# Two attention and MLP layers on one core: part of the softmax exponentials computed on VectorE

## The chip, the cores and the metric

The kernel runs on one core of a Trainium2 chip. The metric is the device time of one launch in microseconds (us). Five engines work side by side, each through its own queue in order: TensorE (PE) multiplies matrices, ScalarE (ACT) evaluates functions such as exp and gelu, VectorE (DVE) does elementwise arithmetic, GpSimd (POOL) does small helpers, and SyncE (SP) starts the DMAs. Data lie in SBUF, results of matmuls in PSUM, which has 8 banks of 128 x 512 fp32. Engines wait for each other through semaphores.

## The reference

One sequence of 2048 tokens with 512 features passes twice through the same two blocks, with the same weights both times. Block A is attention with 32 query heads of 16 features that share one key head and one value head. Block B is a mixer that shifts four quarters of the features along the sequence, and an MLP of width 1792.

```python
def _A_ref(x, wq, wk, wv, wo):
    q = (x @ wq).reshape(B, S, H, Dh).transpose(0, 2, 1, 3)      # H = 32, Dh = 16
    k = x @ wk
    v = x @ wv
    scores = jnp.einsum("bhqd,bkd->bhqk", q, k) * (Dh ** -0.5)
    p = _softmax(scores, axis=-1)
    o = jnp.einsum("bhqk,bkd->bhqd", p, v)
    return o.transpose(0, 2, 1, 3).reshape(B, S, H * Dh) @ wo

def _B_ref(x, w1, w2, w3, w4):
    h = _gelu(_layernorm(x) @ w1)
    hs = (the four quarters of h, shifted by 1, -1, 2, -2 tokens) @ w2
    x1 = x + hs
    return x1 + _gelu(_layernorm(x1) @ w3) @ w4

x = x + _A_ref(_layernorm(x), ...);  x = x + _B_ref(_layernorm(x), ...)    # and both once more
```

The softmax takes 2 x 32 x 2048 x 2048 exponentials, 268 million, for few multiplications around each of them.

## The kernel before

**Tiles and loops.** Queries are taken in four chunks of 512 per layer, heads in eight blocks of four, keys in 16 blocks of 128. One step is a *group*: layer, chunk, head block, key block, written `(la, c, b, kb)` in `make_groups` (line 582). There are 1024 groups. A group has four *tiles*, one for each head of the block: 128 keys by 512 queries of scores. So there are 4096 tiles. A score matmul (line 623) uses only 32 of the 128 rows of TensorE, at row position 32 x head. The four products with the values (line 695) use 32 columns each and run side by side into the accumulator bank 5. The values have a column of ones, so the same products also sum the exponentials. After the last key block of a head block `block_end` (line 704) copies the accumulator to SBUF, takes reciprocals and scales.

**PSUM.** ScalarE has two slots, banks 0 to 2 and banks 3 and 4. `declare_unit` (line 628) fills a slot with three or two tiles and runs one exponential over the whole slot (line 646), into one of four output buffers `EA`. Bank 5 is the accumulator. Banks 6 and 7 are a pool for everything else: projections, transposes, the mixer and the MLP. This *side work* of a chunk (`chunk_end`, line 804) is declared when its attention is done, and it runs during the attention of the chunk after it.

**Who sets the order.** The whole program is planned before it is emitted. `Plan.op` records an operation with its engine, what it reads and writes, a duration and a priority. `Plan.run` simulates the engines with those durations, and puts on each engine the ready operation with the lowest priority number. `Plan.emit` then writes each engine's queue in that order, with the semaphore waits that the dependences need. So at run time the order of every queue is fixed. An operation with `take` needs a free pool bank when it is placed; `give` returns the bank. Score units have priority 0, products with the values 2, normalisation 5, side work 10.

**The feed.** `pump` (line 757) is called as the planned clock advances. While fewer than three of the last four units are unfinished, it opens the next group, puts its tiles on a list and declares units from that list. A group's products are declared as soon as all its four tiles have a place in a unit.

**The switch.** `USE_DVE_EXP` (line 289) is False. It is read in two places. In `memory` (line 344) it allocates the buffers `DJ`, `DF`, `DG` and `ED`. In `pump` (line 770) it calls `consider_pairs` (line 791) when a group is opened, which may call `declare_pair` (line 653). With False neither function runs, and all four tiles of each group go to ScalarE.

Of the kernel before, what the change touches and what calls it, by code (L numbers as in the profile page):

```python
# [281 lines left out]
class Kernel:  # L282
# [3 lines left out]
    ACC = 5  # L286
    POOL_BANKS = (6, 7)
    N_EA = 4
    USE_DVE_EXP = False
    AHEAD = 4  # L290
    MAX_PAIRS = 2

# [7 lines left out]
    def sb(self, name, shape, dtype=dt.bfloat16):  # L300
        n = 1
        for s in shape:
            n *= s
        ap = self.stack.enter_context(self.nc.sbuf_tensor(name, [128, n], dtype))[:, :]
        self.sbytes += n * dt.size(dtype)
        return self.shaped(ap, shape)
# [9 lines left out]
    def memory(self):  # L316
# [26 lines left out]
        self.EA = sb("EA", [self.N_EA, 3, 512])  # L343
        if self.USE_DVE_EXP:
            self.DJ = sb("DJ", [2, 1024], dt.uint16)
# [411 lines left out]
    def pump(self, now):  # L757
# [5 lines left out]
        while True:  # L763
# [4 lines left out]
            while len(self.open_tiles) < nb and self.gi < G:  # L768
                n = self.gi
                if self.USE_DVE_EXP:  # L770
                    self.consider_pairs(now, n)
# [251 lines left out]
```

## Time and profile before

| | |
|---|---|
| time, median of 3 runs | 2240.59 us (2235.44 to 2243.05) |
| time of the profiled execution | 2245.48 us |
| its span, first to last instruction | 2243.3 us |
| mean granted clock of TensorE | 0.69 |
| ScalarE busy | 1990.5 us, 89% |
| TensorE busy | 1864.3 us, 83% |
| VectorE busy | 485.5 us, 22% |
| GpSimd busy | 65.7 us, 3% |

"Busy" is the time in which at least one instruction of the engine runs; on TensorE, whose matmuls are pipelined and overlap, a busy engine need not be at its peak. The granted clock is the share of TensorE's full clock that the chip allowed; the same matmul takes longer at 0.5 than at 1.0. A line of costly instructions gives the source line, engine and operation, the shapes, the count, then busy time and mean duration in nanoseconds of one, then the idle time of the engine just before them and what ended it. A line of a stretch gives its start and end, its length, the busy time of PE, weight loads, DVE, ACT and POOL with counts, the granted clock, the DMA share and GB/s. A line in order of time gives the start, the duration, the engine, the source line and the count of instructions merged in it.

### The profile page before, as it was taken

How to read it: one execution, taken by the hardware profiler on the slowest of the kernel's cores; microseconds unless marked ns; L12 is line 12 of the kernel's file. 1: busy time of each engine (PE TensorE's matmuls, PEld its weight loads, DVE VectorE, ACT ScalarE, POOL GpSimd, SP SyncE). 2: the span in 40 equal slices, each digit the busy share in tenths (PEclk: the TensorE clock that was granted, in tenths of full speed). 3: DMA queues.
4: the chain of work that ended last, by engine and by line, in shares of the span. 5: the costliest groups of instructions: out<-in, count | busy, mean ns of one | idle time of the engine just before them, and what ended most of it. 6: DMA issues, size and time to landing. Idle time of an engine off the chain costs nothing.

```text
span 2243.3 us, 26540 instructions
## 1 busy us (share of the span) xinstructions
PE 1864.3 (83%) x11836; PEld 490.0 (22%) x11836; DVE 485.5 (22%) x931; ACT 1990.5 (89%) x1699; POOL 65.7 (3%) x133
## 2 busy tenths in 40 slices
PE   6777898878888798887879789887888878887867
PEld 2111122211222122221222122221122212221123
DVE  6000032201422024210232124200142002310033
ACT  2999998999999998999999989899998999899931
POOL 3000000000000000000000000000000000000000
PEclk9555597755886578855689568765597756695568
DMA  4000000000000000000000000000000000000000
GB/s 142 1 1 1 1 1 1 1 1 1 1 1 1 1 1 1 1 1 1 1 1 1 1 1 1 1 8 1 1 1 1 10 1 1 1 8 3 1 1 12
DMA packets 10145, 11.68 MB, mean 5 GB/s; under 512 B 1584, under 2 KB 9520, under 8 KB 10032
## 3 DMA queue, kind: packets, MB, share of 16 engines
q1 hardware_dynamic: 10032, 10.00, 1.4%
q8 instruction: 92, 1.51, 0.3%
q14 instruction: 21, 0.17, 0.0%
HBM read 7.90 MB, written 2.10 MB: 4 GB/s over the span
## 4 chain that ended last, share of the span: by engine, by line
ACT 59%; PE 36%; DVE 2%; POOL 1%; issue 1%; ACTq 0%; POOLq 0%
ACT EA L646 55%; PE PB L623 12%; PE PB L695 8%; PE PB L946 4%; PE PB L971 3%; PE PB L843 3%; PE PB L570 2%; ACT G L958 2%; PE PB L913 1%; PE PB L487 1%; ACT L646 1%; PE PB L877 1%; ACT GP L885 1%; PE PB L530 1%; PE PB L741 0%
## 5 line engine op out<-in xcount | busy, mean ns | idle before, releaser
L646 ACT ACTIVATE EA<-PB 128x1536 bf16<-128x1536 f32 (+1 forms) x1639 | 1883.4, 1254 | 166.6 <-PE PB L695 87.1
L623 PE MATMUL PB<-QT,KT 32*128 32x512 bf16 x4096 | 857.3, 518 | 257.3 <-ACT EA L646 252.9
L695 PE MATMUL PB<-EA,VP 128*32 128x512 bf16 x4096 | 545.5, 523 | 1.8 <-DVE ACCF L719 1.3
L623 PEld LDWEIGHTS PB<-QT,KT 32*128 32x128 bf16 x4096 | 164.4, 96 | 943.5 <-ACT EA L646 882.5
L719 DVE CAST ACCF<-PB 128x512 bf16<-128x512 f32 x57 | 39.4, 692 | 835.9 <-PE PB L695 835.9
L695 PEld LDWEIGHTS PB<-EA,VP 128*32 128x32 bf16 x4096 | 110.7, 98 | 368.3 <-issue 357.7
L971 PE MATMUL PB<-W,G 128*128 128x512 bf16 x448 | 140.5, 436 | 52.9 <-ACT G L958 52.9
L946 PE MATMUL PB<-ZT,W 128*128 128x384 bf16 (+2 forms) x560 | 134.6, 364 | 1.5 <-DVE ZT L494 0.7
L951 DVE CAST G<-PB 128x512 bf16<-128x512 f32 (+2 forms) x140 | 81.7, 584 | 122.4 <-PE PB L946 121.5
L958 ACT ACTIVATE G<-G 128x2688 bf16<-128x2688 bf16 (+2 forms) x20 | 50.7, 2584 | 46.1 <-DVE G L951 46.0
L570 PE MATMUL PB<-YT,WQ 128*128 128x512 bf16 x256 | 83.0, 443 | 0.0
L843 PE MATMUL PB<-WO,OT 128*128 128x512 bf16 x256 | 72.3, 402 | 0.8 <-DVE OT L747 0.8
L575 DVE CAST QT<-PB 128x512 bf16<-128x512 f32 x64 | 43.8, 687 | 133.0 <-PE PB L570 132.6
L487 PE MATMUL PB<-IDENT,ZR 128*128 128x128 bf16 x384 | 44.8, 271 | 30.4 <-DVE ZR L507 14.2
L913 PE MATMUL PB<-W,GP 128*128 128x512 bf16 x128 | 49.5, 521 | 21.6 <-ACT GP L885 20.9
L747 DVE TENSOR_TENSOR OT<-ACCF,PB 128x512 bf16<-128x512 bf16 x64 | 44.0, 687 | 100.4 <-PE PB L741 100.2
L463 POOL TENSOR_SCALAR SM<-MV 128x4 f32<-128x4 f32 (+3 forms) x29 | 6.8, 234 | 2010.4 <-DVE MV L448 2010.4
L971 PEld LDWEIGHTS PB<-W,G 128*128 128x128 bf16 x448 | 37.1, 105 | 115.5 <-ACT G L958 55.4
L946 PEld LDWEIGHTS PB<-ZT,W 128*128 128x128 bf16 x560 | 43.8, 101 | 62.0 <-issue 34.3
L446 DVE BATCH_NORM_STATS2 ST<-X 128x6 f32<-128x512 f32 (+1 forms) x64 | 43.5, 688 | 5.1 <-DMA X<-in_A_x_dram 3.6
L877 PE MATMUL PB<-ZT,W 128*128 128x512 bf16 x128 | 40.9, 435 | 0.8 <-DVE ZT L494 0.8
L487 PEld LDWEIGHTS PB<-IDENT,ZR 128*128 128x128 bf16 x384 | 30.0, 120 | 52.9 <-issue 14.6
(66 smaller groups left out, 557.3 us busy)
## 6 DMA issues: line engine op xcount, KB each, us to landing
W<-in_B_w_dram SPq DMA_DIRECT2D x2, 1792.0 KB, 13.8
X<-in_A_x_dram SPq DMA_DIRECT2D x8, 256.0 KB, 6.1
out_dram<-OUTB SPq DMA_DIRECT2D x16, 128.0 KB, 1.7
W<-in_B_w_dram SPq DMA_DIRECT2D x2, 512.0 KB, 8.0
G<-in_A_wq_dram SPq DMA_DIRECT2D x1, 512.0 KB, 5.6
WO<-in_A_wo_dram SPq DMA_DIRECT2D x4, 128.0 KB, 2.7
G<-in_A_wk_dram SPq DMA_DIRECT2D x1, 16.0 KB, 4.6
WV<-in_A_wv_dram SPq DMA_DIRECT2D x1, 16.0 KB, 14.7
```

Source lines behind the costliest of these rows:

```text
L487: ins = e.transpose(self.PBH[:, L.bank, j * 512 + i * 128:j * 512 + (i + 1) * 128], self.ZR[:, tb % 4, dc * 128:(dc + 1) * 128], self.IDENT)
L570: ins = e.matmul(self.PB[:, L.bank, :], lhsT=self.WQ[:, b, dc, :], rhs=self.YT[:, slot, dc, :], start=(dc == 0), stop=(dc == 3))
L623: return e.matmul(self.PB[:, bank, :], lhsT=self.KT[32 * h:32 * h + 32, la, kb * 128:(kb + 1) * 128], rhs=self.QT[32 * h:32 * h + 32, c % ...
L646: o = op("ACT", lambda e: e.activation(self.EA[:, ea, 0:n, :], self.PB[:, b0:b0 + n, :], ACTF.Exp, scale=0.25), writes=[("BK", b0), ("EA", ...
L695: ins = e.matmul(self.PB[32 * h:32 * h + 32, self.ACC, :], lhsT=self.VP[:, la, kb, :], rhs=e4[h][0], start=first, stop=(end is not None), ...
L843: ins = e.matmul(self.PB[:, L.bank, :], lhsT=self.OT[:, b, q:q + 128], rhs=self.WO[:, b, :], start=(b == 0), stop=(b == 7))
L877: ins = e.matmul(self.PB[:, L.bank, :], lhsT=self.W1[:, dc, f * 128:(f + 1) * 128], rhs=ZT[:, dc, :], start=(dc == 0), stop=(dc == 3))
L913: ins = e.matmul(self.PB[:, L.bank, :], lhsT=self.GP[:, par, f, a:a + 128], rhs=self.W2[:, f, :], start=(f == 0), stop=(f == 3))
L946: ins = e.matmul(self.PB[:, L.bank, 0:n], lhsT=self.W3[:, dc, f * 128:(f + 1) * 128], rhs=ZT[:, dc, 0:n], start=(dc == 0), stop=(dc == 3))
L951: op("DVE", lambda e, f=f, L=L: e.tensor_copy(self.G2[:, f, 0:n], self.PB[:, L.bank, 0:n]), writes=[L, ("G2", f)], dur=t_ps(n), give=L)
L958: ins = e.activation(self.G2[:, a:a + 7, 0:n], self.G2[:, a:a + 7, 0:n], ACTF.Gelu_apprx_tanh)
L971: ins = e.matmul(self.PB[:, L.bank, :], lhsT=self.G2[:, f, i * 128:(i + 1) * 128], rhs=self.W4[:, f, :], start=(f == 0), stop=False)
```

## The change

One constant is turned over:

```diff
@@ class Kernel
     ACC = 5
     POOL_BANKS = (6, 7)
     N_EA = 4
-    USE_DVE_EXP = False
+    USE_DVE_EXP = True
     AHEAD = 4
     MAX_PAIRS = 2
```

With that, `pump` asks `consider_pairs` at each group. It walks two groups at a time, up to four groups ahead of the one that is opened, and declares a pair if fewer than two of the last six pairs are unfinished on the planned clock:

```python
while self.dve_gi < n + self.AHEAD and self.dve_gi + 1 < G:
    d = self.dve_gi
    self.dve_gi += 2
    live = sum(1 for o in self.pairs[-6:] if not (o.placed and o.end <= now + 1e-9))
    if live < self.MAX_PAIRS and d >= n:
        self.declare_pair(d)
```

A pair is the tile of head 3 of two groups that follow each other. Each of the two tiles takes a pool bank and a score matmul of its own, and VectorE does the rest:

```python
# twice, one tile each:  J = uint16(score * 128 * log2(e) / 4 + 127 * 128)      PSUM -> SBUF, 512 wide
e.tensor_scalar(out=self.DJ[:, js, i * 512:(i + 1) * 512], in0=self.PB[:, L.bank, :],
                scalar1=128 * LOG2E * 0.25, scalar2=float(127 * 128), op0=ALU.mult, op1=ALU.add)
# then once for both tiles, 1024 wide, SBUF -> SBUF:
e.tensor_scalar(out=self.DF, in0=J, scalar1=0x7F, scalar2=None, op0=ALU.bitwise_and)       # mantissa bits
e.tensor_scalar(out=self.DG, in0=self.DF, scalar1=-129.0, scalar2=0.33 / 128, op0=ALU.add, op1=ALU.mult)
e.tensor_tensor(out=self.DG, in0=self.DF, in1=self.DG, op=ALU.mult)
e.tensor_tensor(out=(self.ED as uint16), in0=J, in1=self.DG, op=ALU.add)                   # bits of a bf16
```

`J` holds the bits of a bf16 number whose exponent is right and whose mantissa is the linear fraction; the last three operations add a quadratic correction to the mantissa. `DJ` has two buffers, `ED` three, `DF` and `DG` one each. In the planner the four wide operations have durations of 0.33, 0.33, 0.6 and 0.6 us, the two PSUM reads `t_ps(512)` = 0.667 us each and the score matmul 0.27 us; the matmul has priority 1, the VectorE operations 2. The products of a group whose head 3 is in a pair read that tile from `ED` instead of `EA`, so they also wait for the pair's last operation. Nothing else in the code changes, but since the planner places every operation anew, the order of all queues changes.

## The prediction

> **What bounds the kernel now.** I read the page first: engine shares, the slices, the chain that ended last, the costliest groups.
>
> ```profile
> span 2243.3 us, 26540 instructions
> ...
> PE 1864.3 (83%) x11836; PEld 490.0 (22%) x11836; DVE 485.5 (22%) x931; ACT 1990.5 (89%) x1699; POOL 65.7 (3%) x133
> ...
> PEclk9555597755886578855689568765597756695568
> ...
> ACT 59%; PE 36%; DVE 2%; POOL 1%; issue 1%; ACTq 0%; POOLq 0%
> ...
> L646 ACT ACTIVATE EA<-PB 128x1536 bf16<-128x1536 f32 (+1 forms) x1639 | 1883.4, 1254 | 166.6 <-PE PB L695 87.1
> L623 PE MATMUL PB<-QT,KT 32*128 32x512 bf16 x4096 | 857.3, 518 | 257.3 <-ACT EA L646 252.9
> L695 PE MATMUL PB<-EA,VP 128*32 128x512 bf16 x4096 | 545.5, 523 | 1.8 <-DVE ACCF L719 1.3
> ```
>
> ScalarE is busy 89% of the span, and 1883.4 of its 1990.5 us are the exponentials of 4096 tiles of 128x512: 0.46 us a tile. VectorE is busy 22%. TensorE is the second engine: 83% busy, at a granted clock that falls to 0.5 in many slices. Next come stretches of the trace: head, middle and tail, then single stages.
>
> ```profile
> 0.00:45.00 45.00, 26.64 (x157) 11.24 (x158) 32.88 (x74) 5.91 (x5) 18.33 (x36) 1.00 0.55 176
> 45.00:2148.00 2103.00, 1771.56 (x11370) 449.50 (x11370) 410.37 (x773) 1974.07 (x1689) 41.77 (x86) 0.68 0.01 1
> 2148.00:2243.30 95.30, 66.08 (x311) 29.30 (x311) 42.29 (x86) 10.52 (x6) 5.59 (x11) 0.80 0.02 7
> ...
> 825.00:850.00 25.00, 24.34 (x190) 7.66 (x189) 13.90 (x29) 24.86 (x23) 3.33 (x6) 1.00 0.00 1
> 1000.00:1025.00 25.00, 19.78 (x129) 4.20 (x125) 1.63 (x3) 24.30 (x22) 0.00 (x0) 0.50 0.00 1
> 1081.00:1092.00 11.00, 10.84 (x61) 2.42 (x61) 1.55 (x4) 8.48 (x8) 0.00 (x0) 0.50 0.00 0
> 1092.00:1098.00 6.00, 6.00 (x42) 1.72 (x41) 2.59 (x6) 5.10 (x5) 0.00 (x0) 0.96 0.01 3
> ```
>
> The columns are the stretch, its length, busy time (and count) of PE, weight loads, DVE, ACT and POOL, then the granted clock. The 140 us of head and tail hold no attention to speak of. In the middle ScalarE works 1974 of 2103 us. There are two kinds of stage: attention alone (1000 to 1025: clock 0.50, VectorE nearly idle) and attention with the projections and the MLP of the chunk before it (825 to 850: clock 1.00, TensorE full). From 1081 to 1092 TensorE is full at 0.50 and ScalarE is busy only 8.48 of 11 us: there TensorE sets the pace. What a group of matmuls costs at each clock is in the order of instructions:
>
> ```profile
> 1003.05 0.61 PE L623 MATMUL PB<-QT,KT 32*128 32x512 bf16 x3 [0.19 <-ACT EA L646]
> 1003.59 0.62 PE L695 MATMUL PB<-EA,VP 128*32 128x512 bf16 x4
> ...
> 830.56 0.39 PE L623 MATMUL PB<-QT,KT 32*128 32x512 bf16 x3
> 830.88 0.40 PE L695 MATMUL PB<-EA,VP 128*32 128x512 bf16 x4
> ...
> 701.77 1.03 PE L623 MATMUL PB<-QT,KT 32*128 32x512 bf16 x5
> ```
>
> From start to start a group of three score matmuls takes 0.54 us at clock 0.50 and 0.32 at 1.00.
>
> **The change, part by part.** The switch lets every pair of consecutive key blocks hand head 3 of both (two tiles) to VectorE. Per pair it takes two tiles from ScalarE and adds two single score matmuls in a pool bank (6 or 7), two VectorE reads of PSUM into uint16, one AND and one affine on 1024 elements, one multiply and one add of two tensors of 1024. It adds no DMA. The two probability-times-value groups (L695) of the pair now also wait for the add.
>
> *How many pairs.* Each two key blocks bring one chance, 512 in all; it is taken when fewer than two earlier pairs are unfinished on the planner's clock. By the planner's own durations a pair takes 0.667x2 + 0.33x2 + 0.6x2 = 3.19 us of VectorE, 3.47 with four self-latencies of 0.07; I take 3.33. VectorE's other work is 485.5/512 = 0.95 us for each two blocks. ScalarE gives two blocks 8 x 0.46 = 3.68 us plus its other (1990.5 - 1883.4)/512 = 0.2, less 0.92 for a taken pair. With a share f taken, 3.33f + 0.95 = 3.88 - 0.92f, so f = 0.69: 350 pairs. By stage f could be from 0.5 to 0.85, so 260 to 430.
>
> *ScalarE.* 700 tiles x 0.46 = 322 us less (240 to 395). If nothing else came to bind, the span would be 2243 - 322 = 1921.
>
> *VectorE.* No row has an integer operation, or two tensors from SBUF. The nearest rows:
>
> ```profile
> L951 DVE CAST G<-PB 128x512 bf16<-128x512 f32 x56 | 38.7, 692 | 68.4 <-PE PB L946 68.4
> L951 DVE CAST G<-PB 128x256 bf16<-128x256 f32 x28 | 11.8, 423 | 9.8 <-PE PB L946 9.7
> L494 DVE COPY ZT<-PB 128x1024 bf16<-128x1024 bf16 x24 | 16.5, 689 | 19.3 <-PE PB L487 19.1
> L494 DVE COPY ZT<-PB 128x512 bf16<-128x512 bf16 x4 | 1.7, 422 | 1.2 <-PE PB L487 1.1
> L932 DVE TENSOR_SCALAR ZR<-Y,MV,SM 128x512 bf16<-128x512 bf16 x32 | 11.3, 408 | 8.7 <-POOL SM L465 8.6
> L862 DVE TENSOR_SCALAR ZR<-Y,SM 128x512 bf16<-128x512 bf16 x32 | 9.1, 346 | 1.4 <-POOL SM L465 1.4
> ...
> 579.83 0.68 DVE L575 CAST QT<-PB 128x512 bf16<-128x512 f32 x1
> 580.43 1.13 DVE L862 TENSOR_SCALAR ZR<-Y,SM 128x512 bf16<-128x512 bf16 x4
> ...
> 605.17 0.69 DVE L446 BATCH_NORM_STATS2 ST<-Y 128x6 f32<-128x512 bf16 x1
> 605.90 0.18 DVE L448 BATCH_NORM_AGGREGATE MV<-ST 128x2 f32<-128x6 f32 x1
> ```
>
> The casts give a fixed 0.154 us and 1.05 ns an element, the 16-bit copy half of that per element. The two scalar rows differ by 0.062 us for one more scalar from memory; with none, L862 would be 0.284, so 0.25 ns an element. The PSUM reads are the 0.69 row. The AND and the affine are from 0.154 + 1024 x 0.25 = 0.41 to 0.154 + 1024 x 1.05 = 1.23 us each; the multiply and the add from 0.69 (the copy of 1024) to 1.23. Every tensor there has 16-bit elements, as in the fast rows, so I take the low values: 2x0.69 + 2x0.41 + 2x0.69 = 3.58 us a pair, with the high ones 6.3. An independent instruction starts some 0.08 us before the end of the one ahead (579.83 + 0.68 against 580.43), a dependent one 0.04 after it (605.86 against 605.90). So a pair alone takes 3.58 - 0.08 + 4 x 0.04 = 3.66, one interleaved with other work about 3.1; I take 3.4. 350 pairs are 1190 us, and VectorE comes to 1676, 82% of a span of 2045. Its slack covers it, but no longer loosely.
>
> [...]
>
> *TensorE.* Score units of 3 and 2 tiles fall from 1639 to (4096 - 700)/2.5 = 1358, and 700 single matmuls come: 419 more groups. A single one lies between nothing (beside a unit in another row group) and a whole group, 0.32 to 0.54; behind another unit it adds 1.03 - 0.61 = 0.42 us. Bounds: 700 x 0 - 281 x 0.43 = -121 us, and 419 x 0.54 = +226. I take 419 x 0.43 = +180, nearest to the row of five. At the present mix of clocks TensorE then needs 1772 + 180 = 1952 us in the middle, 2092 with head and tail, against 1921 on ScalarE's path. So TensorE is full next, and how far its clock rises decides between the two.
>
> *The fixed order.* Each queue is written out from the planner's durations. A lone pair on the chip, 3.66, is 0.2 us over the planned 3.47. The wait stands ahead of L695 on TensorE; behind it are the next score units, and ScalarE waits for those. Such a wait is hidden while ScalarE has units in its two PSUM slots and four output buffers; uncovered it is 350 x 0.2 = 70 us, so 1991. L695 has these waits today:
>
> ```profile
> ACT EA L646 <- PE PB L695: 87.1, 138, 19.9
> ACT EA L646 <- PE PB L623: 73.9, 68, 19.4
> ```
>
> *Sum.* Between 1991 (ScalarE's path and late pairs) and 2092 (TensorE at today's clocks) I take the middle, 2042; with the 2.2 us that the profiled execution has beside its span (2245.48 against 2243.3), **2045 us**. The profiled execution is 5 us over the median of the runs, 2240.59, which is less than any term here.
>
> **Rivals.** *1. TensorE warms up and ScalarE stays the bound: 1921.* For it: after 1092 the clock stands at 0.96 once TensorE was full. Against it: between 1081 and 1092 a full TensorE stayed at 0.50 for 11 us, and with pairs the attention stage is dense but not full. [...]
>
> *2. The pair is late, and its wait replaces the work removed: slower, 2350.* Place: the wait ahead of L695. Removing two tiles saves 0.92 us a pair, so from 0.92 us of uncovered waiting per pair the change loses. If each pair comes late by one foreign VectorE instruction (0.69) and a group on a cold TensorE that got in front of its score matmuls (0.54), that is 1.23 x 350 = 430 us on 1921. For it: three engines would run at 80 to 95% in a fixed order, planned with score groups of 0.33 us where the chip takes 0.54 in the cold stage, and two pool banks serve pairs and projections. Against it: pairs are declared up to four key blocks ahead.
>
> *3. VectorE becomes the bound, because its integer operations run one element at a time: slower, 2550.* If the AND, the multiply and the add run unpacked, a pair is 3.4 + 0.82 + 2 x 0.54 = 5.3 us; VectorE's middle is 410 + 350 x 5.3 = 2265, and at the 94% that ScalarE reaches in the middle now, 2410 + 140 = 2550. The change loses from (2103 x 0.94 - 410)/350 = 4.5 us a pair; the AND alone unpacked (4.2) gives 2140. For it: no row shows such an operation packed.
>
> *4. Few pairs are taken: 2240.* If side work keeps both pool banks in the planner, pairs stay unfinished and are skipped. Against it: pairs go ahead of side work in every queue.
>
> **How the numbers follow.** Forecast (1991 to 2140, all of it faster): 0.42. Rival 1 (1900 to 1990): 0.13. Rival 2: 0.22, with 0.03 of it still faster. Rival 3: 0.16. Rival 4: 0.07, of which 0.05 is no change. A measurement of this kernel tells about 0.3% from no change. Faster: 0.42 + 0.13 + 0.03 + 0.01 = 0.59; same 0.05; slower 0.19 + 0.16 + 0.01 = 0.36. The range that leaves out two in ten runs from 1935 (part of rival 1) to 2400 (rival 2, not the most of rival 3). The likeliest case's own range is 1991 to 2140.
>
> **What the profile after would show.** The count of the uint16 AND gives the pairs (260 to 430), and its mean its mode: near 410 ns packed, near 1230 not. ScalarE's exponentials should fall to about 1560 us, VectorE should rise to about 1680, TensorE's share over 90% with fewer slices at 0.5. If ScalarE's idle time grows by more than 322 us, ended by L623 or L695 whose own wait is for the add of L679, rival 2 is right; if VectorE is above 94%, rival 3. The prediction is wrong if the time is not below 2234, or if the gain is there with fewer than 200 pairs.

## The result, and the profile after

The changed kernel takes 1965.72 us (median of 4 runs, 1959.47 to 1972.42) against 2240.3 us for the kernel before. The ratio is 0.8777, with an interval of 0.8742 to 0.8812: 12.2% faster. The forecast was 2045 with a range of 1935 to 2400, so the time lies inside the range, 79 us under the forecast. It lies outside the likeliest case's own range of 1991 to 2140, in the stretch that the prediction gave to its first rival. One of the five runs of experiment 6 and one of the kernel before fell into a slower state; medians count them, ratios leave them out.

The page of the changed kernel, with the lines that answer to those shown of before:

```profile
span 1960.9 us, 28291 instructions
...
PE 1704.8 (87%) x11706; PEld 483.7 (25%) x11836; DVE 1618.1 (83%) x3091; ACT 1660.2 (85%) x1409; POOL 73.8 (4%) x133
...
PEclk9655588777757997689877867877897898967898
...
ACT 45%; PE 38%; DVE 13%; POOL 2%; issue 1%; ACTq 0%; POOLq 0%
...
L646 ACT ACTIVATE EA<-PB 128x1536 bf16<-128x1536 f32 x1351 | 1555.7, 1273 | 209.2 <-PE PB L623 153.2
L623 PE MATMUL PB<-QT,KT 32*128 32x512 bf16 x4096 | 774.9, 469 | 128.1 <-ACT EA L646 100.6
L665 DVE TENSOR_SCALAR DJ<-PB 128x512 uint16<-128x512 f32 x720 | 488.0, 685 | 115.4 <-PE PB L623 112.7
...
L677 DVE TENSOR_TENSOR DG<-DF,DG 128x1024 bf16<-128x1024 uint16 x360 | 246.2, 684 | 4.5
L679 DVE TENSOR_TENSOR ED<-DJ,DG 128x1024 uint16<-128x1024 uint16 x360 | 245.9, 683 | 4.1
...
L671 DVE TENSOR_SCALAR DF<-DJ 128x1024 uint16<-128x1024 uint16 x360 | 151.6, 421 | 4.2
L674 DVE TENSOR_SCALAR DG<-DF 128x1024 bf16<-128x1024 uint16 x360 | 150.8, 419 | 4.4
```

Read it in this order. The count of L671 is the number of pairs, 360. The four wide operations take 0.42 and 0.68 us, near the low values of the prediction (0.41 and 0.69). ScalarE's work falls by 1990.5 - 1660.2 = 330.3 us. The span falls by only 2243.3 - 1960.9 = 282.4, so ScalarE's idle time (span less busy) grew by 47.9 us, from 252.8 to 300.7. And TensorE, whose score matmuls now come in more and smaller groups, is busy for *less* time than before, with fewer slices of the clock line at 5 (4 of 40, where it was 15). The page says 1704.8 us, but only 11706 of the 11836 matmuls are in this trace. A second profile of the same kernel (beside experiment 7) has them all: 1747.0 us in a span of 1976.9, which is 117.3 us less than before. All three engines now stand between 82% and 88%.

The attention-only stage, first before and then after, as stretches of 150 us (columns as in the prediction):

```profile
100.00:250.00 150.00, 120.27 (x735) 24.73 (x731) 8.18 (x15) 144.42 (x128) 0.00 (x0) 0.50 0.00 1
```

```profile
100.00:250.00 150.00, 143.54 (x898) 30.05 (x896) 138.89 (x255) 142.94 (x124) 0.00 (x0) 0.51 0.00 1
```

At the same half clock TensorE goes from 80% to 96% busy and VectorE from 5% to 93%, while ScalarE stays at 95 to 96%. In this stage the three are nearly full together.

Where did ScalarE's extra idle time arise? Its waits around the boundary of the two layers, before (1060 to 1340 us):

```profile
ACT EA L646 <- PE PB L623: 15.2, 16, 1.8
ACT EA L646 <- PE PB L695: 4.9, 11, 1.4
```

and after, for about the same stage (900 to 1160 us of the shorter span):

```profile
ACT EA L646 <- PE PB L623: 50.1, 16, 18.6
ACT G L958 <- DVE G L951: 7.5, 2, 5.3
ACT EA L646 <- PE PB L695: 3.4, 4, 1.9
```

The columns are total us, times and longest. 61 us in place of 20: that is 41 of the 48. Between the same two groups, from the products of group 512 to those of group 620 (counted from 0), ScalarE idles for 16.6 us before and for 64.1 after. One wait alone lasts 18.6 us, and what TensorE did shortly before it ended shows the reason:

```profile
1137.25 1.89 PE L487 MATMUL PB<-IDENT,ZR 128*128 128x128 bf16 x16 [5.13 <-DVE ZR L507]
1140.33 1.49 PE L530 MATMUL PB<-YT,WK 128*128 128x512 bf16 x3 [1.19 <-DVE YT L494]
1142.60 1.04 PE L623 MATMUL PB<-QT,KT 32*128 32x512 bf16 x7 [0.36 <-DVE KT L536]
```

The score matmuls (L623) wait for keys of the second layer (`KT`), whose projection (L530) waits for the transposes (L487) and the normalisation ahead of them. With attention faster, the second layer asks for keys that the side work has not yet delivered. In the page's busy line of ScalarE, slices 20 and 23 to 24 of the 40 show it as a dip (5, 7 and 5 tenths busy, where the other slices of the attention have 8 or 9).

### The profile page after: what moved, and what is told of

Read it like the earlier page. It is cut to its first block, busy times and chain, and to the rows that moved or that the text cites. A ratio compares the mean times of both kernels' runs of the same rounds, so it can differ in the third digit from the quotient of the medians.

```text
span 1960.9 us, 28291 instructions
## 1 busy us (share of the span) xinstructions
PE 1704.8 (87%) x11706; PEld 483.7 (25%) x11836; DVE 1618.1 (83%) x3091; ACT 1660.2 (85%) x1409; POOL 73.8 (4%) x133
## 4 chain that ended last, share of the span: by engine, by line
ACT 45%; PE 38%; DVE 13%; POOL 2%; issue 1%; ACTq 0%; POOLq 0%
ACT EA L646 41%; PE PB L623 14%; PE PB L695 8%; DVE DJ L665 4%; PE PB L971 3%; PE PB L946 3%; PE PB L570 2%; ACT G L958 2%; PE PB L487 2%; PE PB L843 2%; DVE DG L677 1%; DVE ED L679 1%; DVE DF L671 1%; PE PB L877 1%; DVE DG L674 1%
## 5 line engine op out<-in xcount | busy, mean ns | idle before, releaser
L646 ACT ACTIVATE EA<-PB 128x1536 bf16<-128x1536 f32 x1351 | 1555.7, 1273 | 209.2 <-PE PB L623 153.2
L623 PE MATMUL PB<-QT,KT 32*128 32x512 bf16 x4096 | 774.9, 469 | 128.1 <-ACT EA L646 100.6
L665 DVE TENSOR_SCALAR DJ<-PB 128x512 uint16<-128x512 f32 x720 | 488.0, 685 | 115.4 <-PE PB L623 112.7
L695 PE MATMUL PB<-EA,VP 128*32 128x512 bf16 x3376 | 487.4, 473 | 7.0 <-DVE ACCF L719 3.6
L623 PEld LDWEIGHTS PB<-QT,KT 32*128 32x128 bf16 x4096 | 165.0, 94 | 706.3 <-ACT EA L646 477.7
L695 PE MATMUL PB<-ED,VP 128*32 128x512 bf16 x720 | 335.1, 471 | 0.0
L677 DVE TENSOR_TENSOR DG<-DF,DG 128x1024 bf16<-128x1024 uint16 x360 | 246.2, 684 | 4.5
L679 DVE TENSOR_TENSOR ED<-DJ,DG 128x1024 uint16<-128x1024 uint16 x360 | 245.9, 683 | 4.1
L695 PEld LDWEIGHTS PB<-EA,VP 128*32 128x32 bf16 x3376 | 104.0, 96 | 347.8 <-issue 307.9
L671 DVE TENSOR_SCALAR DF<-DJ 128x1024 uint16<-128x1024 uint16 x360 | 151.6, 421 | 4.2
L674 DVE TENSOR_SCALAR DG<-DF 128x1024 bf16<-128x1024 uint16 x360 | 150.8, 419 | 4.4
L946 PE MATMUL PB<-ZT,W 128*128 128x384 bf16 (+2 forms) x534 | 133.3, 362 | 8.7 <-issue 3.9
L843 PE MATMUL PB<-WO,OT 128*128 128x512 bf16 x237 | 72.6, 421 | 6.0 <-issue 2.6
L487 PE MATMUL PB<-IDENT,ZR 128*128 128x128 bf16 x384 | 46.7, 283 | 30.0 <-DVE ZR L507 20.5
L695 PEld LDWEIGHTS PB<-ED,VP 128*32 128x32 bf16 x720 | 67.4, 96 | 0.0
```

The lines of the kernel that those rows point to most:

```text
L623: return e.matmul(self.PB[:, bank, :], lhsT=self.KT[32 * h:32 * h + 32, la, kb * 128:(kb + 1) * 128], rhs=self.QT[32 * h:32 * h + 32, c % ...
L646: o = op("ACT", lambda e: e.activation(self.EA[:, ea, 0:n, :], self.PB[:, b0:b0 + n, :], ACTF.Exp, scale=0.25), writes=[("BK", b0), ("EA", ...
L665: op("DVE", lambda e, L=L, i=i: e.tensor_scalar(out=self.DJ[:, js, i * 512:(i + 1) * 512], in0=self.PB[:, L.bank, :], scalar1=128 * LOG2E ...
L671: op("DVE", lambda e: e.tensor_scalar(out=self.DF, in0=J, scalar1=0x7F, scalar2=None, op0=ALU.bitwise_and), reads=jt, writes=[("DF",)], du ...
L674: op("DVE", lambda e: e.tensor_scalar(out=self.DG, in0=self.DF, scalar1=-129.0, scalar2=0.33 / 128, op0=ALU.add, op1=ALU.mult), reads=[("D ...
L677: op("DVE", lambda e: e.tensor_tensor(out=self.DG, in0=self.DF, in1=self.DG, op=ALU.mult), reads=[("DF",), ("DG",)], writes=[("DG",)], dur ...
```

## The experiments

Three theories were set against each other. **A**: ScalarE stays the bound, the others are hidden. **B**: TensorE is the bound. **C**: late pairs, and so VectorE, hold up the products and through them ScalarE. Times are medians, ratios are to the kernel before on the same chip.

**1. Half of the pairs.**

```diff
-            if live < self.MAX_PAIRS and d >= n:
+            if live < self.MAX_PAIRS and d >= n and d % 4 == 0:
```

> Only every second chance may take a pair: 255 pairs in place of 360, the rest of the code as after the change. Theory A (ScalarE stays the bound; each pair is worth its two tiles less some waiting, 282 us / 360 = 0.78 us): 2240 - 255 x 0.78 = 2041 us, in a straight line with 0 and 360 pairs. Theory B (TensorE is the bound in the changed kernel, so the last pairs gain little): 1970 to 2000 us. Theory C (late pairs, waited for by the products, cost more the fuller VectorE is): below the straight line, about 2010 us.

Measured: 2009.34 us, ratio 0.8971 (0.8937 to 0.9004). Against 2242.3 on the same chip 255 pairs, spread over the program, save 233 us, 0.91 us each, which is the whole of two tiles on ScalarE (0.92). ScalarE's idle time is 2007.5 - 1754.7 = 252.8 us, as before the change. The 105 pairs more of the changed kernel save 43.6 us more, 0.42 each. Theory A's straight line (2041) is wrong, and B's range is missed by 9 us; C's number, 2010, fits, but experiment 3 speaks against C. Something takes more than half of what the last pairs give.

**2. TensorE's part alone.** ScalarE keeps every tile. The single score matmuls are added, VectorE's operations cover two columns, and nothing uses what they compute.

```diff
-        for i in range(2):
-            self.dve_of[n + i] = (self.ED[:, es, i, :], ("ED", es))
...
+            if live < self.MAX_PAIRS and d >= n and self.npair < 360 * (d + 2) // G:
...
-                out=self.DJ[:, js, i * 512:(i + 1) * 512], in0=self.PB[:, L.bank, :],
+                out=self.DJ[:, js, i * 512:i * 512 + 2], in0=self.PB[:, L.bank, 0:2],
```

> The kernel before, with TensorE's part of the change alone: ScalarE keeps all 4096 tiles, and 360 times two further single score matmuls go into pool banks. VectorE reads only two columns of each and does its four wide operations on two columns; nothing uses the result. Theory A (TensorE's added work is hidden under ScalarE, because singles run beside a unit and the clock rises when TensorE gets denser): 2240 to 2260 us, with a higher granted clock than 0.69. Theory B (it is exposed, as the prediction's term of 180 us at today's clocks has it): 2330 to 2420 us, clock about 0.69. Theory C says nothing here: as A.

Measured: 2299.36 us, ratio 1.0256 (1.0217 to 1.0295), clock 0.716. It is between A and B: the part is exposed, but by 57 us. The page:

```profile
span 2298.4 us, 30145 instructions
...
PE 1997.4 (87%) x12556; PEld 520.0 (23%) x12556; DVE 773.1 (34%) x3091; ACT 1996.4 (87%) x1699; POOL 65.8 (3%) x134
...
L624 PE MATMUL PB<-QT,KT 32*128 32x512 bf16 x4816 | 989.6, 501 | 179.9 <-ACT EA L647 161.6 <-DVE DJ L666 1.0 <-DVE QT L576 0.9
```

In this trace the score matmuls form 2183 groups (those that start within 30 ns of each other count as one), against 1641 before: 542 more. TensorE's busy time grows by 133 us, 0.25 per group, at a mean clock of 0.716 in place of 0.690, and the kernel gets 57 us longer. The singles take their pool banks here as in the change, and side work may wait for those; what that adds to the 57 us was not measured apart. In the changed kernel the same count gives 1834 groups, 193 more than before: there ScalarE's units shrink in number (1351 in place of 1639), so some 240 of the 720 singles run beside a unit.

**3. VectorE's part taken out of the changed kernel.** The order of all queues stays; the two PSUM reads and the four wide operations cover two columns, and `ED` is filled with ones once at the start.

```diff
-        op("DVE", lambda e: e.tensor_scalar(out=self.DF, in0=J, scalar1=0x7F, scalar2=None,
+        op("DVE", lambda e: e.tensor_scalar(out=self.DF[:, 0:2], in0=J[:, 0:2], scalar1=0x7F, scalar2=None,
... (the other five alike)
```

> The changed kernel with the same order of all queues, but VectorE's work of the pairs nearly gone: the two reads of PSUM and the four wide operations cover two columns each, so the output isn't the reference's. Theory A (ScalarE is the bound and VectorE has slack): 1940 to 1965 us, at most 1.3% under the changed kernel. Theory B (TensorE): 1960 to 1970 us. Theory C (late pairs hold up the products and through them ScalarE): 1900 us or less, near ScalarE's path of 2243 - 328 = 1916.

Measured: 1970.78 us, ratio 0.8791 (0.8748 to 0.8834): no difference from the changed kernel (0.8742 to 0.8812), with VectorE busy 732.8 us in place of 1618.1. Theory C is wrong. At 83% VectorE's work costs nothing that these runs can tell, which is to about 12 us. Theories A and B both foresaw about this, so the run does not part them.

**4. and 5. More VectorE work per pair.** One kernel does each pair's last add twice (first into a spare buffer); the other puts a maximum over the 1024 elements ahead of it. The order of all queues is that of the changed kernel. (The diff shows both kernels at once; each has one of the two marked lines.)

```diff
+        def fadd(e):
+            e.tensor_tensor(out=self.DH[:, 0, :], in0=J, in1=self.DG, op=ALU.add)                   # add_1more
+            e.tensor_reduce(out=self.DR, in_=self.DG, axis=mybir.AxisListType.X, op=ALU.max)        # red_1
+            return e.tensor_tensor(out=(self.ED as uint16), in0=J, in1=self.DG, op=ALU.add)
```

> The changed kernel with the same order of all queues, but a maximum over the 1024 elements (into one unused element) ahead of each pair's last add: some 1.15 us more of VectorE per pair, so 4.5 in place of 3.4, which the prediction named as the point from which the change loses. VectorE's middle would be 1540 + 360 x 1.15 = 1954 us. The prediction's rival 3 (VectorE's work over the share of 94% that ScalarE reached): 2220 us, the whole gain gone. Theory A with VectorE's slack used to the last: 1954 + 140 = 2095 us. Theory B (TensorE the bound): under 2060 us.

> The changed kernel with the same order of all queues, and each pair's last add done twice (into a spare buffer first): 0.6 us more of VectorE per pair, 4.0 in place of 3.4. The prediction's point from which VectorE takes all is 4.5. If VectorE's slack absorbs it up to a share of 94% of the middle (1540 + 360 x 0.6 = 1756 of 1821 is 96%): 1980 to 2010 us. If each further us of VectorE counts fully from the first one: 1966 + 216 = 2180 us.

Measured: 2094.24 us with the second add, ratio 0.9349 (0.9325 to 0.9374); 2249.14 us with the maximum, ratio 1.0037 (1.0017 to 1.0057). The lines of the page with the maximum:

```profile
PE 1869.8 (83%) x11836; PEld 490.0 (22%) x11836; DVE 2011.6 (90%) x3451; ACT 1692.0 (75%) x1409; POOL 69.5 (3%) x133
...
L681 DVE TENSOR_REDUCE DR<-DG 128x1 bf16<-128x1024 bf16 x360 | 436.8, 1213 | 4.0
```

Busy time per pair, as (VectorE busy - 485.5)/360, is 0.69 us in experiment 3, 3.15 in the changed kernel, 3.72 with the second add and 4.24 with the maximum. From 0.69 to 3.15 the time does not move. From 3.72 to 4.24 (187 us in all) it moves by 155 us, 0.83 for one. Drawn back at that slope, the line meets 1966 us at 3.3 us a pair. So by this estimate, a line through two kernels with different added instructions, the changed kernel stands 0.15 us a pair under the point where VectorE begins to count. At 4.24, a share of only 90%, the whole gain is gone. Of the forecasts only the prediction's rival (2220) came near for the maximum; for the second add, 1980 to 2010 and 2180 both missed. The waits of ScalarE for score matmuls, and of these for VectorE's read of PSUM (total us, times, longest), show how, first in the changed kernel, then with the maximum:

```profile
ACT EA L646 <- PE PB L623: 153.2, 139, 19.6
...
PE PB L623 <- DVE DJ L665: 10.8, 31, 0.8
```

```profile
ACT EA L647 <- PE PB L624: 372.6, 382, 19.7
...
PE PB L624 <- DVE DJ L666: 93.8, 109, 2.9
```

ScalarE waits 382 times in place of 139. A pair's score matmul needs a pool bank, and the bank comes free when VectorE has read it into `DJ`. So the matmul waits at the head of TensorE's queue, which is in order, and ScalarE's next scores stand behind it. With the second add the same row has 49.3 us, 86 times, between the two. The mean clock fell too, to 0.719 with the maximum and 0.761 with the second add, from 0.78 to 0.79 in the changed kernel: which part of the loss came through the clock, these runs do not tell.

**6. and 7. The layer boundary.** No pairs while the first 77 groups of the second layer are fed; run twice, the second time beside the changed kernel itself.

```diff
-            if live < self.MAX_PAIRS and d >= n:
+            if live < self.MAX_PAIRS and d >= n and not (self.groups[d][0:2] == (1, 0) and n < 512 + 77):
```

> The changed kernel without pairs while the first 77 groups of the second layer's first chunk are fed (337 pairs in all), so that pool banks and VectorE are free there for the side work that the second layer waits for. Theory A (ScalarE's path plus a stall at the layer boundary, where it waits for score matmuls some 50 us in 900 to 1160): 23 pairs fewer cost 21 us, the stall shrinks by 30 to 45: 1940 to 1960 us. Theory B (TensorE's load decides everywhere): 1966 to 1985 us.

> no_pairs_at_boundary once more, beside the changed kernel on one chip. Its stall at the layer boundary was 27 us shorter and its 23 pairs fewer cost 21 us of ScalarE. If both only add up: 0 to 10 us under the changed kernel here. If the stall's time comes back elsewhere (TensorE at a lower clock): 10 to 25 us over it.

> The changed kernel itself, on the chip of the three runs beside it. Stages with the same order of all queues took up to 2% longer in kernels that differ only later, with the granted clock lower. If that is the chip or the run, this comes out at 1965 to 1985 us; if not, at 1960 to 1972.

Measured: 1984.51 us, ratio 0.8845 (0.8823 to 0.8866); the second time 1976.91, ratio 0.8821 (0.8803 to 0.8839), beside 1967.62, ratio 0.8774 (0.8749 to 0.8799), for the changed kernel. So by the medians it is 9 us slower. The first time says less: that execution was already 7 us behind the second profile of the changed kernel at group 500 (919.6 against 912.6 us), where the order of all queues is still the same. ScalarE's waits at the boundary, in the changed kernel on that chip and in this one (920 to 1180 us):

```profile
ACT EA L646 <- PE PB L623: 54.0, 21, 19.4
ACT G L958 <- DVE G L951: 7.5, 2, 5.3
ACT EA L646 <- PE PB L695: 3.4, 4, 1.9
```

```profile
ACT EA L646 <- PE PB L623: 29.5, 16, 13.9
ACT EA L646 <- PE PB L695: 3.3, 6, 1.3
```

The stall falls from 65 to 33 us, and ScalarE's exponentials grow by 23 us for 23 pairs fewer. That should leave 9 us of gain, and by the medians there are 9 us of loss. The two profiled executions, 1978.66 and 1977.72 us, show the place: the products of group 660 start at 1258.8 us in the changed kernel and at 1246.6 in this one, so behind the boundary it is 12 us ahead. From there to the end it loses 11 of them, at a mean clock of 0.80 against 0.83. What drove that clock was not found out.

**8. and 9. Fewer groups of score matmuls.** One kernel takes heads 3 and 2 for a pair, the other also lets the planner hold a single until a unit was placed just before it.

```diff
-            g = self.groups[n + i] + (3, n + i)
+            g = self.groups[n + i] + (3 - i, n + i)
... and, in the planner's choice for TensorE (beside_units):
+                if o.kind == "single" and not self.beside(t) and t < o.ready + 1.0:
+                    skipped.append(item)
+                    continue
```

> The changed kernel, but the second tile of a pair is that of head 2 and not of head 3, so that a pair's two score matmuls lie in different row groups of TensorE and can run side by side. The planner's numbers are the same. Theory A: 1960 to 1968 us, nothing gained where TensorE doesn't bind. Theory B: TensorE's groups of score matmuls fall by some 50 to 100, 0.43 us each: 1925 to 1950 us.

> As two_heads, and the planner holds a single score matmul up to 1 us until a score unit was placed just before it, and counts it 0.05 us there. In the plan 516 of 724 singles then run beside a unit, so TensorE loses some 200 more groups, 90 us of work. Theory A (ScalarE and the boundary decide): 1950 to 1970 us. Theory B (TensorE): 1900 to 1930 us.

Measured: 1983.07 us, ratio 0.8844 (0.8820 to 0.8868), and 1975.96, ratio 0.8825 (0.8796 to 0.8854). Neither is faster than the changed kernel on that chip (1967.62 us, 0.8749 to 0.8799), and all four forecasts were too low. Both left the groups nearly as they were: 1827 and 1795 against 1834 in the changed kernel. In the second, by this count, some 280 of the 724 singles run beside a unit, where the plan had 516. What the planner puts side by side is often not side by side on the chip, so these two say nothing on whether fewer groups would help.

**10. Both ideas together.**

> beside_units and no_pairs_at_boundary together. Theory A: 1930 to 1955 us, the boundary's gain and little more. Theory B: 1900 to 1930 us, TensorE's gain and none for the boundary.

Measured: 1963.40 us, ratio 0.8784 (0.8750 to 0.8819), with 1791 groups: no difference from the changed kernel, and above both forecasts. No version here beats it.

**11. TensorE relieved.** The products with the values cover half of the queries, except in the first key block of each head block. The order of all queues is that of the changed kernel.

```diff
+                w = 512 if first else 256
-                ins = e.matmul(self.PB[32 * h:32 * h + 32, self.ACC, :], lhsT=self.VP[:, la, kb, :], rhs=e4[h][0],
+                ins = e.matmul(self.PB[32 * h:32 * h + 32, self.ACC, 0:w], lhsT=self.VP[:, la, kb, :], rhs=e4[h][0][:, 0:w],
```

> The changed kernel with the same order of all queues, but the products with the values cover 256 of 512 queries in all key blocks except the first of each head block, so the output isn't the reference's. TensorE loses some 960 x 0.107 (full clock) to 960 x 0.21 us (half clock), about 150 us. Theory A (ScalarE's path and the layer boundary are the bound): within 0.7% of the changed kernel. Theory B (TensorE, most of all at half clock, still holds ScalarE up): 1900 to 1940 us.

Measured: 2022.13 us, ratio 0.9032 (0.9006 to 0.9058): with less to do, the kernel is 54 us *slower* than the changed one on the same chip. Both theories are wrong on this one. First the changed kernel on that chip, then this one:

```profile
PE 1747.0 (88%) x11836; PEld 485.3 (25%) x11836; DVE 1620.0 (82%) x3091; ACT 1662.2 (84%) x1409; POOL 73.2 (4%) x133
...
PEclk9655587777857997779878758867797888978899
...
L623 PE MATMUL PB<-QT,KT 32*128 32x512 bf16 x4096 | 777.2, 471 | 130.3 <-ACT EA L646 104.2
```

```profile
PE 1782.0 (88%) x11836; PEld 495.1 (24%) x11836; DVE 1626.5 (80%) x3091; ACT 1669.1 (82%) x1409; POOL 73.3 (4%) x133
...
PEclk9555577666776795667757856755666677766698
...
L623 PE MATMUL PB<-QT,KT 32*128 32x512 bf16 x4096 | 851.9, 520 | 146.4 <-ACT EA L646 122.5 <-DVE DJ L665 8.7 <-DVE KT L536 2.0
```

The granted clock fell from 0.781 to 0.685. The products got shorter: from 149 to 156 us, in the stage at clock 0.51, a group of four takes 0.40 us with 256 columns and 0.61 to 0.62 with 512, which agrees with the 0.21 us of the expectation. (The 0.107 at full clock is near half of what one more 512-wide matmul added there in the kernel before: from 831 to 833 us two of L843 take 0.60 us, four take 1.04.) But the score matmuls, untouched, take 851.9 us in place of 777.2, and the side work slows with them: a matmul of L946 takes 432 ns on average, where it took 362 in the first profile of the changed kernel (which has 534 of the 560). ScalarE's waits for score matmuls go from 164.8 to 208.1 us. So a slower TensorE does hold ScalarE up here, and it was slower at a lower clock (a score matmul 520 ns on average in place of 471). Why the clock fell is not shown.

## Why the prediction was right or wrong, point by point

**The number.** The direction was right, and the change works by the mechanism that was forecast: tiles leave ScalarE, and VectorE's slack takes them. The time fell inside the wide range but not inside the likeliest case's own, because the terms for TensorE and for the wait behind late pairs were too large for what they stood for. Of the signs that were named, 360 pairs, the AND (421 ns against 410) and the exponentials (1555.7 us) came as forecast; TensorE's share stayed at 87 to 88% and did not pass 90%.

**Pairs and ScalarE: right.** 350 pairs were forecast from the balance of the planner's durations, 360 came; 322 us less work on ScalarE, 327.7 (1883.4 - 1555.7) in the exponentials.

**VectorE: right in kind and size.** The low value was taken for each operation by element width: 0.41 and 0.69 us, measured 0.42 and 0.68. The sum said 1676, the page says 1618: a pair costs 3.15 us of busy time, at the interleaved end (3.1) of the two and not at 3.4. The estimate, taken from rows with bf16, came out for uint16 too: 421 ns for the bitwise operation, 419 for the affine from uint16 to bf16, 684 and 683 for the two that mix uint16 and bf16. "Its slack covers it" was true, and by the line drawn in experiments 4 and 5 with little to spare: 3.15 against 3.3 us a pair. The point from which rival 3 loses, 4.5 us, was about 4.24.

**TensorE: the term that was mis-sized.** The step "419 x 0.43 = +180, at the present mix of clocks 2092" put one end of the sum at 2092. Two things in it were off. The change brought 193 more groups and not 419, because some 240 singles ran beside a unit, where the value taken let each of them stand alone; at 0.43 us that is 83 us and not 180. And the mix of clocks did not stay: 0.690 before, 0.787 after. With both, TensorE's busy time went down, from 1864.3 to 1747.0 in the complete profile. Why the clock rose is not shown. Taking the middle between the two ends was then too high: 2042 against a span of 1960.9.

**The fixed order: near in size by luck, wrong in place.** 70 us of uncovered waiting were put at the wait of L695 for the pair's add. ScalarE's idle time did grow, by 48 us, but hardly there:

```profile
  PEld PB L695: 5.2, 13
...
  PE PB L695: 1.0, 2
```

These rows, the time that the products spent waiting for the tile `ED` in the changed kernel, give 6 us for all of them together. ScalarE itself waits 32.0 us behind products that read `ED`, but 25.6 of these are one wait at the start of attention, where it waited 19.9 us before and by then the first pair had been done for some 23 us. 41 of the 48 us are at the boundary of the layers, which the prediction did not look at: the side work there had been just in time, and attention got faster.

**Rivals.** The first (ScalarE stays the bound, 1921) came nearest, 45 us under the time; its condition, a higher clock of TensorE, is what happened in the mean (0.690 to 0.787), though in the attention-only stage the clock stood at 0.50 from 125 to 245 us with TensorE busy for 115.12 of these 120 us. The second (late pairs) fell: L695 waits 6 us, and without VectorE's work the time is the same. The third was right that VectorE can take the whole gain, as the kernel with the maximum shows, but its condition, 1.23 us each for the AND, the multiply and the add, did not hold: the first took 0.42, the others 0.68. The fourth fell with 360 pairs.

**What is settled and what is open.** The gain is two tiles of ScalarE per pair, and with 255 pairs spread over the program it comes in full. That 105 more give less than half each is shown, and that ScalarE's added idle time lies for the most part at the layer boundary. The cause is not shown part by part: more work on TensorE lengthened the kernel by 57 us (experiment 2), a lower clock came with 54 us more (experiment 11), and shortening the stall at the boundary did not shorten it.

## What to carry to other kernels

When work moves from a full engine to an idle one, price the small helpers that it drags along on the third engine, and look for the stage where that one is full. A fixed order is planned for one speed of each engine: the work of an engine at 83% cost nothing that could be measured here, at 90% the whole gain was gone, so find the point where it begins to cost by adding work, and don't read slack off the busy share. And when a stage gets faster, look at what had been just in time for it, at the boundaries first.

## What was not expected of the hardware

TensorE's granted clock did not follow its busy share here. In the changed kernel it stood at 0.50 from 125 to 245 us with TensorE 96% busy:

```profile
125.00:245.00 120.00, 115.12 (x720) 23.78 (x718) 112.02 (x207) 115.64 (x100) 0.00 (x0) 0.50 0.00 1
```

With half of the columns of most value products left out, the busy share was 88% as before, but the mean clock went from 0.781 to 0.685 and the kernel became 54 us slower. In experiment 2, with score matmuls added, it was higher (0.716 against 0.690). So with work added TensorE's clock was higher than in the kernel without it, and with work taken away it was lower, and the time longer. What the clock goes by, these runs don't tell.
